# Moving the Winograd operand sums of an attention-plus-MLP kernel from VectorE to GpSimd

## The chip, the cores and the metric

The kernel runs on one core of one Trainium2 chip. The metric is the device time of one execution in microseconds (us); lower is better. The kernel before took 890.3 us in the median of three runs (887.12, 890.3 and 890.57 us). One further execution was recorded with a profile; all rows below are from that one. The engines are called by the profile's short names: PE (TensorE matmul), PEld (its weight loads), DVE (VectorE), ACT (ScalarE), POOL (GpSimd), SP (the queue that issues DMAs here).

## The reference

Attention with softmaxes on q and k apart, then an MLP whose activation is `h * erf(softplus(h))`. Shapes: 8 batches, 8 heads, 576 positions, head size 64; so 4608 tokens of 512 features, and weights of 512x2048 and 2048x512, all float32.

```python
q_s = softmax(q, over d);  k_s = softmax(k, over the sequence)
kv  = einsum('bhsd,bhse->bhde', k_s, v)
x   = einsum('bhsd,bhde->bhse', q_s, kv) as (4608, 512)
h   = x @ w_in
g   = h * erf(max(h, 0) + log1p(exp(-|h|)))
out = g @ w_out
```

## The kernel before, in words

**Tiling.** Tokens are worked in 12 blocks of 384 (three blocks for each pair of batches; `NBK` is 3), and the 2048 hidden features in 4 groups of 512. One item n is a block with a group, so there are 48 items: items 0 to 3 are block 0, items 4 to 7 block 1, items 8 to 11 block 2. Per item, `mm1` makes h for 512 features and 384 tokens, ACT does softplus and erf, DVE multiplies and splits g (lines 933, 946, 950), and `mm2` (line 978) adds to the output tiles.

**Precision.** Block 0 runs in float32 (`mm1_32`, and line 969) while the weights still arrive and are decoded. From block 1 on, each operand is split into a float16 high part and a float16 low part by `split2`: ACT writes the high part (line 268), DVE the low part, from the float32 source and the high part (line 269). Each product then takes three float16 matmuls.

**Seven products in place of eight.** From block 1 on, `mm1` multiplies a 2x2 grid of weight blocks with a 2x2 grid of x blocks in Winograd's form, with seven products (names `pX`, `pY`, `pZ` for the PSUM banks, line 854). For this, sums of the blocks are needed on both sides. On the weights' side `wsplit(jn)` splits the plain blocks A00, A01 and A11, and then line 294 forms four sums in place, each of 128x512 float32, in a chain: A11 = A10 + A11, A10 = A00 - A10, A00 = A11 - A00, A01 = A01 - A00. `wsplit_sums(jn)` splits the four results. This happens once for each of the four groups of `w_in` (jobs 0, 1, 3 and 5 of `JOBS`): 16 sums. On the side of x, `finish(0)` splits the plain blocks of an x block, and `finish(1)` forms four sums in place at line 360, each of 128x384 float32, and splits them: 4 sums for each of blocks 1 to 11, 44 in all. An in-place sum has to come after every split that reads the old value, and the splits of the sums after it.

**Where they stand in the order.** The list `ORDER` gives the sequence in which the program emits its parts, and a planner in the framework lays out each engine's queue from it, so neighbours in a queue can belong to different parts. Each queue is worked in order. After `Z` (the weights' scales) come `S0` (wsplit of job 0), `R0` (wsplit_sums of job 0), `f0 f1` (finish of block 1), `S1 R1`, and later, from `SPLITS`, S3 R3 and S5 R5; S2, S4, S6 and S7 are the splits of `w_out`, which have no sums. Block 2's finish is emitted in item 6. Between them stand the steps of attention for the next batches (`A`), on the same engines.

**Products and what they read.** In `mm1`, part k = 0 reads plain blocks alone; part k = 1 begins with the product that reads weight operand 6 and x operand 3, both sums. DVE also adds the products up in PSUM and SBUF (lines 866, 868, 876, 879), and ACT copies some (871, 873, 881). POOL does little: it clears tiles (lines 105 and 550) and does one subtraction of the first batch (line 740).

Of the kernel before, what the change touches and what calls it, by code (L numbers as in the profile page):

```python
# [13 lines left out]
ALU = mybir.AluOpType  # L14
# [39 lines left out]
def attn_moe_kernel(  # L54
# [9 lines left out]
    nc = tc.nc  # L64
# [15 lines left out]
    NBK = PT // T  # L80
# [122 lines left out]
    def whalf(jn, h):  # L203

        return WT[jn][:, h * 2048:(h + 1) * 2048]

    def wop(jn, h, i, n):

        o = h * WIN + i * 512
        return WT[jn][:, o:o + n * 512].rearrange("p (n c f) -> p n c f", n=n, c=2)  # L210
# [56 lines left out]
    def split2(src, hi, lo, s):  # L267
        nc.scalar.activation(hi, src, AF.Copy, scale=s)  # L268
        nc.vector.scalar_tensor_tensor(lo, src, s, hi, op0=ALU.mult, op1=ALU.subtract)  # L269
# [3 lines left out]
    def wsplit(jn):  # L273


        which, g = wjobs[jn]
        s = w_s[which][:, g:g + 1]
        assert "all" in wready and not raws and jn == nsplit[0]
        nsplit[0] += 1
        if which == "out":  # L280
            split2(stg.pop(jn), whalf(jn, 0), whalf(jn, 1), s)
            wdone(jn)
            return
        sg = stg[jn].rearrange("p (c f) -> p c f", c=4)
        A = {(i, j): sg[:, 2 * j:2 * j + 2, 256 * i:256 * i + 256]
             for i in range(2) for j in range(2)}
        hi, lo = (wop(jn, h, 0, 2).rearrange("p n c f -> p (n c) f") for h in range(2))
        split2(sg[:, :, :256], hi, lo, s)
        split2(A[1, 1], wop(jn, 0, 2, 1)[:, 0], wop(jn, 1, 2, 1)[:, 0], s)
        for o, x, y, op in (  # L290
            ((1, 1), (1, 0), (1, 1), ALU.add), ((1, 0), (0, 0), (1, 0), ALU.subtract),
            ((0, 0), (1, 1), (0, 0), ALU.subtract), ((0, 1), (0, 1), (0, 0), ALU.subtract),
        ):
            nc.vector.tensor_tensor(A[o], A[x], A[y], op=op)

    def wsplit_sums(jn):
        which, g = wjobs[jn]
# [8 lines left out]
    def wdone(jn):  # L306
        wready.add(wjobs[jn])
# [33 lines left out]
    def finish(k):  # L341


        i = x_next[0]
        x = xbl[i]
        Th = T // 2
        if k == 0:
            assert i < 3 or ("m", mm1_last[i - 2], 3) in emitted
            x7[i] = xp.tile([P, 2, 7, 2, Th], F16, tag="x7", name=f"x7_{i}")
            hi, lo = (x7[i][:, h, 0:2].rearrange("p n c t -> p (n c) t") for h in range(2))  # L350
            split2(x[:, :, :Th], hi, lo, 1.0)
            split2(x[:, 2:, Th:], x7[i][:, 0, 2], x7[i][:, 1, 2], 1.0)
            return
        Bk = {(d, j): x[:, 2 * d:2 * d + 2, Th * j:Th * j + Th]
              for d in range(2) for j in range(2)}
        for o, a, b in (
            ((0, 0), (0, 1), (0, 0)), ((0, 1), (1, 1), (0, 1)),
            ((1, 1), (1, 1), (0, 0)), ((1, 0), (1, 0), (1, 1)),
        ):
            nc.vector.tensor_tensor(Bk[o], Bk[a], Bk[b], op=ALU.subtract)  # L360
        for j in range(2):
            hi, lo = (
                x7[i][:, h, 3 + 2 * j:5 + 2 * j].rearrange("p n c t -> p (n c) t")
                for h in range(2)
            )
            split2(x[:, :, Th * j:Th * j + Th], hi, lo, 1.0)
        x_next[0] += 1
# [637 lines left out]
    def tok(name):  # L1005
# [19 lines left out]
        if c == "w":  # L1025
            warm(*x)
        elif c == "D":
            wdecode(NPC * x[0] + x[1])
        elif c == "Q":
            wsquares(*x)  # L1030
        elif c == "S":
            wsplit(*x)
        elif c == "R":
            wsplit_sums(*x)
        elif c == "f":
            xready(x_next[0])
            finish(x[0] % 2)
        elif c == "Z":
            wscales()
        elif c == "m":  # L1040
            (mm1_32 if x[0] < NG else mm1)(*x)
            emitted.add(("m", *x))
        elif c == "M":
            mm2(*x)
            emitted.add(("M", *x))
        else:
            fn[c](*x)
# [82 lines left out]
```

## Time and profile before

| | |
|---|---|
| median of three runs | 890.3 us (887.12 to 890.57) |
| profiled execution: own time | 886.76 us |
| its span, first to last instruction | 884.9 us |
| mean granted TensorE clock | 0.992 of full |
| PE busy | 832.7 us (94%) |
| DVE busy | 656.9 us (74%) |
| ACT busy | 504.5 us (57%) |
| POOL busy | 6.4 us (1%), 14 instructions |

The busy shares are means over stages: the beginning (loads, decoding, block 0), a stage from about 124 to 185 us in which the weights and blocks 1 and 2 are split, and the long rest. The rows below give the stages apart. A stretch of idle time is named with the instruction that ended it.

### The profile page before, as it was taken

The numbers are of one execution on the slowest core, as the hardware profiler recorded it, in microseconds if no ns is written. First come the engines' busy times: TensorE is split into PE (matmuls) and PEld (weight loads), VectorE is DVE, ScalarE is ACT, GpSimd is POOL, SyncE is SP. The second block draws the span as 40 slices with busy tenths as digits, with TensorE's granted clock in tenths as the row PEclk, the third lists the DMA queues.
The fourth block names the chain that finished last, engine by engine and source line by source line (L and its number), as shares of the span: only waits on it lengthen the run. The fifth ranks groups of instructions, "written<-read, shape, count | busy, mean of one in ns | idle before, by whom it ended". The sixth has DMA issues, their size and how long they took to land.

```text
span 884.9 us, 15492 instructions
## 1 busy us (share of the span) xinstructions
PE 832.7 (94%) x6556; PEld 573.0 (65%) x6556; DVE 656.9 (74%) x908; ACT 504.5 (57%) x645; POOL 6.4 (1%) x14
## 2 busy tenths in 40 slices
PE   2899995799989999999999999999999999999997
PEld 1555554566667667767777667667777677676763
DVE  7899589998977796786886596777885575644453
ACT  2468567866475646645745646645745646553632
POOL 2000000000000000000000000000000000000000
PEclk9999998899999999999999999999999999999999
DMA  9983711022104111311033111311010000000100
GB/s 272 361 238 81 224 45 51 2 66 60 49 25 102 48 49 27 89 48 25 13 74 77 37 49 33 76 48 26 13 49 1 13 24 2 24 13 1 36 1 36
DMA packets 117380, 55.52 MB, mean 63 GB/s; under 512 B 106560, under 2 KB 108608, under 8 KB 117312
## 3 DMA queue, kind: packets, MB, share of 16 engines
q1 hardware_dynamic: 117312, 54.54, 22.6%
q8 instruction: 51, 0.84, 0.4%
q14 instruction: 17, 0.14, 0.0%
HBM read 45.09 MB, written 9.44 MB: 62 GB/s over the span
## 4 chain that ended last, share of the span: by engine, by line
PE 65%; DVE 20%; ACT 10%; issue 3%; DMA 1%; SPq 1%; ACTq 0%; DVEq 0%
PE o L978 26%; PE pX L854 14%; PE pZ L854 7%; ACT G L316 5%; ACT L316 4%; PE o L969 3%; PE pY L854 3%; DVE G L933 3%; PE kv L502 3%; PE pX L893 2%; DVE H L950 2%; DVE kmax L458 2%; DVE wt L269 2%; PE qT L577 1%; PE pY L893 1%
## 5 line engine op out<-in xcount | busy, mean ns | idle before, releaser
L978 PE MATMUL o<-wt,H 128*128 128x512 f16 x1584 | 366.1, 379 | 1.9 <-DVE H L946 1.3
L854 PEld LDWEIGHTS <-wt 128*128 128x128 f16 x3696 | 311.5, 98 | 49.1 <-issue 26.3
L978 PEld LDWEIGHTS <-H 128*128 128x128 f16 x1584 | 152.5, 98 | 156.4 <-DVE H L946 1.8
L854 PE MATMUL pX<-x,wt 128*128 128x192 f16 x2112 | 205.9, 247 | 12.6 <-DVE H L876 7.2
L316 ACT ACT_TABLE_LOAD x104 | 133.4, 1283 | 7.0 <-DVE H L879 5.3
L933 DVE SCALAR_TENSOR_TENSOR G<-G,small,H 128x1536 f32<-128x1536 f32 x44 | 80.0, 1818 | 69.3 <-ACT G L316 69.0
L854 PE MATMUL pZ<-x,wt 128*128 128x192 f16 x1056 | 105.5, 249 | 9.3 <-ACT x L268 5.8
L881 ACT COPY H<-pX 128x384 f32<-128x384 f32 x44 | 21.0, 477 | 148.0 <-PE pX L854 143.1
L316 ACT ACTIVATE G<-H,U 128x768 f32<-128x768 f32 (+1 forms) x60 | 73.0, 1232 | 22.7 <-DVE H L879 22.1
L950 DVE TENSOR_TENSOR H<-G,H 128x1536 f16<-128x1536 f32 x44 | 77.3, 1756 | 1.1
L316 ACT ACTIVATE G<-G 128x1536 f32<-128x1536 f32 x48 | 71.2, 1484 | 0.5
L854 PE MATMUL pY<-x,wt 128*128 128x192 f16 x528 | 51.1, 246 | 0.0
L404 ACT ACTIVATE x<-x 128x384 f32<-128x384 f32 (+1 forms) x52 | 17.7, 386 | 55.0 <-PE x L589 52.8
L866 DVE COPY H<-pY 128x384 f32<-128x384 f32 x44 | 24.4, 554 | 30.5 <-PE pY L854 30.5
L946 DVE CAST H<-G 128x1536 f16<-128x1536 f32 x44 | 42.1, 956 | 0.8
L268 ACT ACTIVATE x<-x 128x768 f16<-128x768 f32 (+1 forms) x44 | 33.0, 763 | 15.3 <-DVE x L360 15.3
L269 DVE SCALAR_TENSOR_TENSOR x<-x,x 128x768 f16<-128x768 f32 (+1 forms) x44 | 37.3, 850 | 5.3 <-ACT x L268 5.1
L994 DVE TENSOR_SCALAR ob<-o,V 128x512 f32<-128x512 f32 x29 | 21.7, 748 | 23.8 <-PE o L978 23.8
L879 DVE TENSOR_TENSOR H<-pZ,H 128x384 f32<-128x384 f32 x44 | 24.2, 551 | 18.0 <-PE pZ L854 18.0
L868 DVE TENSOR_TENSOR H<-pX,H 128x384 f32<-128x384 f32 x44 | 24.4, 555 | 14.4 <-PE pX L854 14.2
L360 DVE TENSOR_TENSOR x<-x 128x384 f32<-128x384 f32 x44 | 24.3, 552 | 4.9 <-ACT x L404 4.5
L458 DVE TENSOR_REDUCE kmax<-k 128x256 f32<-128x1024 f32 x14 | 27.6, 1980 | 0.0
(158 smaller groups left out, 814.6 us busy)
## 6 DMA issues: line engine op xcount, KB each, us to landing
out_dram<-ob SPq DMA_DIRECT2D x32, 256.0 KB, 2.2
vbuf<-in_v_dram SPq DMA_DIRECT2D x60, 128.0 KB, 3.0
wt<-in_moe_w_out_dram SPq DMA_DIRECT2D x7, 1024.0 KB, 9.4
q<-in_q_dram SPq DMA_DIRECT2D x56, 128.0 KB, 2.9
k<-in_k_dram SPq DMA_DIRECT2D x56, 128.0 KB, 3.1
wt<-in_moe_w_in_dram SPq DMA_DIRECT2D x5, 1024.0 KB, 8.7
raw<-in_moe_w_in_dram SPq DMA_DIRECT2D x3, 1024.0 KB, 8.6
H_raw<-in_k_dram SPq DMA_DIRECT2D x2, 512.0 KB, 6.5
```

The costliest lines, as they stand in the source:

```text
L268: nc.scalar.activation(hi, src, AF.Copy, scale=s)
L269: nc.vector.scalar_tensor_tensor(lo, src, s, hi, op0=ALU.mult, op1=ALU.subtract)
L316: i = nc.scalar.activation(out_, in_, func, **kw)
L458: nc.vector.tensor_reduce(kmax[:, hf * 4:hf * 4 + 4, :], ks[hf], axis=AX.X, op=ALU.max)
L502: nc.tensor.matmul(bk[a * D:(a + 1) * D, c * W:(c + 1) * W], kk, vv, start=(t == 0), stop=(t == TM),)
L854: nc.tensor.matmul(o, w[wl][:, c, a * P:(a + 1) * P], x[:, xl, xi, c, :], start=(new and a == 0 and c == 0 and i == 0), stop=(c == 1 and i ...
L893: nc.tensor.matmul(ph[:, :T], w[:, c, a * P:(a + 1) * P], x[:, c, :], start=(c == 0), stop=(c == NC4 - 1),)
L933: nc.vector.scalar_tensor_tensor(flat(s["G"]), flat(s["G"]), GA[:, g:g + 1], flat(s["H"]), op0=ALU.mult, op1=ALU.mult,)
L946: nc.vector.tensor_copy(flat(s["gh"]), flat(s["G"]))
L950: nc.vector.tensor_tensor(flat(s["gl"]), flat(s["G"]), flat(s["gh"]), op=ALU.subtract)
L969: nc.tensor.matmul(o, s["G"][:, a, ts_], w[:, a, :], start=(first_ and a == 0), stop=(last_ and a == FG - 1),)
L978: nc.tensor.matmul(o, s[gt][:, a, ts_], w[wl][:, a, :], start=(first_ and a == 0 and i == 0), stop=(last_ and a == FG - 1 and i == 2),)
```

## The change

The four sums on the weights' blocks are done on GpSimd in place of VectorE, in all four groups. The four sums on an x block are done on GpSimd for blocks 1 and 2, and stay on VectorE for blocks 3 to 11. The operands, the order of emission and everything else stay as they are. So 16 instructions of 128x512 and 8 of 128x384 change their engine.

```diff
@@ wsplit
-            nc.vector.tensor_tensor(A[o], A[x], A[y], op=op)
+            nc.gpsimd.tensor_tensor(A[o], A[x], A[y], op=op)
@@ finish
-            nc.vector.tensor_tensor(Bk[o], Bk[a], Bk[b], op=ALU.subtract)
+            (nc.gpsimd if i < NBK else nc.vector).tensor_tensor(
+                Bk[o], Bk[a], Bk[b], op=ALU.subtract
+            )
```

## Rows read from the trace of the kernel before

**Rows 1.** The stretches of the span (us from its start): length, then busy time and instructions of PE, PEld, DVE, ACT and POOL, then the granted clock of PE (1.00 is 2.4 GHz), the share of the DMA engines and GB/s.

```profile
124.00:134.00 10.00, 10.00 (x49) 5.98 (x48) 9.55 (x18) 9.14 (x17) 0.95 (x1) 1.00 0.49 132
134.00:140.00 6.00, 5.09 (x38) 3.38 (x36) 5.95 (x7) 5.27 (x11) 0.95 (x1) 1.00 0.44 117
140.00:148.00 8.00, 1.04 (x6) 0.78 (x6) 8.00 (x12) 5.41 (x7) 0.00 (x0) 0.76 0.06 13
148.00:172.00 24.00, 16.62 (x150) 14.28 (x149) 24.00 (x25) 17.38 (x20) 0.00 (x0) 0.86 0.00 1
...
300.00:500.00 200.00, 196.84 (x1700) 140.24 (x1699) 151.27 (x211) 115.20 (x142) 0.00 (x0) 1.00 0.21 50
```

**Rows 2.** Who waited for whom from 124 to 172 us: engine, line and what it works on, the one waited for, us in total, times, the longest.

```profile
PE pZ L854 <- ACT x L268: 5.8, 1, 5.8
PE pX L854 <- DVE H L876: 3.2, 2, 2.5
...
PE pZ L854 <- DVE x L269: 1.7, 1, 1.7
PE pZ L854 <- ACT H L871: 1.7, 2, 1.1
...
PE pX L854 <- ACT H L873: 1.5, 2, 1.3
```

**Rows 3.** Instructions around block 1's sums in order of time: start, us, engine, line and operation, and in brackets the idle time before it and what ended it.

```profile
138.84 0.85 ACT L404 ACTIVATE x<-x,x_s 128x128 f32<-128x128 f32 x2
...
141.01 0.55 DVE L269 SCALAR_TENSOR_TENSOR x<-x,x 128x384 f16<-128x384 f32 x1
141.48 0.69 DVE L294 TENSOR_TENSOR wt<-wt 128x512 f32<-128x512 f32 x1
...
144.33 0.84 ACT L268 ACTIVATE x<-x 128x768 f16<-128x768 f32 x1 [0.25 <-DVE x L360]
...
146.28 0.95 DVE L269 SCALAR_TENSOR_TENSOR x<-x,x 128x768 f16<-128x768 f32 x1
...
147.28 1.92 PE L854 MATMUL pZ<-x,wt 128*128 128x192 f16 x11 [1.74 <-DVE x L269]
```

**Rows 4.** The chain of work that ended last, the pieces from 110 to 200 us in order of time: start, us, what. Nine pieces of it are line 294 (the first and the last stand here) and three are line 360 (the first and the last).

```profile
130.70 3.33 DMA q<-in_q_dram
...
136.46 0.60 DVE wt L294
...
140.62 0.47 DVE x L360
...
143.83 0.47 DVE x L360
...
169.48 2.09 PE pX L854 x12
...
179.80 0.60 DVE wt L294
```

**Rows 5.** Line 294 and line 360 over the whole span: number, shortest, median and longest duration in ns, first and last start, shape.

```profile
L294 DVE TENSOR_TENSOR wt<-wt x16: 683/685/693, 126.5 to 179.7; 128x512 f32<-128x512 f32 x16
...
L360 DVE TENSOR_TENSOR x<-x x44: 535/552/560, 132.6 to 750.9; 128x384 f32<-128x384 f32 x44
```

**Rows 6.** Instructions at the beginning of the span in order of time, around the one subtraction on POOL.

```profile
8.41 3.81 DVE L458 TENSOR_REDUCE kmax<-H_raw 128x256 f32<-128x1024 f32 x2
8.58 1.90 POOL L740 TENSOR_TENSOR q<-G_raw,q_m 128x1024 f32<-128x1024 f32 x1 [5.38 <-DVE q_m L739]
10.52 1.06 ACT L735 ACTIVATE q<-q 128x1024 f32<-128x1024 f32 x1 [2.19 <-POOL q L740]
```

**Rows 7.** DVE from 124 to 172 us by line and shape: what it writes and reads, number, busy us, mean ns of one, idle time before. Four lines read PSUM and write `H` (866, 868, 876 and 879), with two instructions each; the first and the last of them stand here.

```profile
L269 DVE SCALAR_TENSOR_TENSOR wt<-wt,small,wt 128x1024 f16<-128x1024 f32 x9 | 11.4, 1278 | 0.0
...
L458 DVE TENSOR_REDUCE kmax<-k 128x256 f32<-128x1024 f32 x2 | 4.0, 1990 | 0.0
...
L415 DVE TENSOR_REDUCE q_m<-q 128x16 f32<-128x1024 f32 x1 | 1.2, 1220 | 0.2 <-DMA q<-in_q_dram 0.2
...
L868 DVE TENSOR_TENSOR H<-pX,H 128x384 f32<-128x384 f32 x2 | 1.1, 556 | 0.0
...
L879 DVE TENSOR_TENSOR H<-pZ,H 128x384 f32<-128x384 f32 x2 | 1.1, 552 | 0.0
L946 DVE CAST H<-G 128x1536 f16<-128x1536 f32 x1 | 1.0, 952 | 0.0
...
L472 DVE TENSOR_REDUCE km<-kT 128x4 f32<-128x512 f32 x1 | 0.7, 684 | 0.0
```

**Rows 8.** A later clearing on POOL and the splits that DVE did at that time, in order of time.

```profile
124.39 1.93 DVE L269 SCALAR_TENSOR_TENSOR wt<-wt,small,wt 128x1024 f16<-128x1024 f32 x2
124.46 0.95 POOL L550 MEMSET kvbd<- 128x1024 f16 x1 [113.98 <-DVE Vt L827]
```

**Rows 9.** POOL's first clearing of tiles, when DVE had not begun, by line: number, busy us, mean ns of one.

```profile
L105 POOL MEMSET kvbd<- 128x1024 f16 x2 | 1.9, 952 | 0.0
```

**Rows 10.** PE in order of time in the same stage: two of its groups of twelve matmuls of line 854.

```profile
151.00 1.16 PE L854 MATMUL pX<-x,wt 128*128 128x192 f16 x12
...
172.53 2.13 PE L854 MATMUL pX<-x,wt 128*128 128x192 f16 x12
```

**Rows 11.** The last split that reads the plain blocks of job 1's weights, in the order of time on DVE.

```profile
133.05 0.75 DVE L269 SCALAR_TENSOR_TENSOR wt<-wt,small,wt 128x512 f16<-128x512 f32 x1
```

## The prediction

> **What bounds the kernel now.** I read the time by stretches first [rows 1]. From 300 to 500 us PE is busy 196.84 of 200 us: the rest of the kernel is PE's own work, and whatever is lost before it is added to the end. From 124 to 172 us it is otherwise. From 140 to 148 us PE works 1.04 of 8 us, from 148 to 172 us 16.62 of 24, while DVE is busy 8.00 of 8 and 24.00 of 24. ACT has room there (17.38 of 24). So in this stage one engine, DVE, is full, and it is the stage that holds the changed instructions. The reader should see that DVE's mean over the span (74%) hides this.
>
> The waits say the same from PE's side [rows 2]: 5.8 us for ACT's split of x, 1.7 us for DVE's split of x, 3.2 us for DVE's additions into H, and 1.7 and 1.5 us for ACT's copies of H. The first two are one place: block 1's first product on sums. x of block 1 is complete at 138.84 + 0.85 = 139.69, DVE has still to read it at 141.01, ACT splits the last sums at 144.33, DVE's low part runs from 146.28 to 147.23, and PE goes on at 147.28 [rows 3]. Here DVE works through other things between the steps of one chain.
>
> The chain of work goes almost wholly through DVE from 134 to 169 us; up to 180 us nine pieces of it are line 294 and three are line 360 [rows 4]. Ahead of 134 us it goes through a load of q that ended at 130.70 + 3.33 = 134.03, so DVE's work before that is not what sets the end. Four of the 16 sums on weights, and the first of the four on block 1, lie there [rows 4, 5].
>
> **The change part by part.** Removed from DVE: 16 instructions of 685 ns and 8 of 552 ns [rows 5]. DVE starts the next instruction before the last has ended, so on the chain one counts 0.60 and 0.47 us [rows 4]: 16 x 0.60 + 8 x 0.47 = 13.4 us in all. On the path are 9 x 0.60 + 3 x 0.47 = 6.8 us. The first job's four sums and block 1's first one are hidden behind the load of q, three sums of the last job stand beside softplus and erf on ACT, and block 2's four lie from about 190 us on, where PE has its own work. These twelve give nothing, and cost nothing as long as that cover is there. If PE runs out of work at block 2, its four sums at POOL's price (below) cost at most 4 x (0.71 - 0.47) = 1.0 us.
>
> Added on POOL: the one subtraction of the trace took 1.90 us for 128x1024, with ACT going on 0.04 us after it [rows 6]. By that, 128x512 is 0.95 us and 128x384 is 0.71 us. One takes longer there than on DVE. But POOL does little else in this stage, so the four sums of a job follow one another with nothing between them: 4 x (0.95 + 0.04) = 4.0 us, where job 1's took DVE from 136.46 [rows 4] to 141.48 + 0.69 = 142.17 us [rows 3]. So the splits behind the sums are not late.
>
> No DMA moves. The new waits are at POOL's sums (for the splits that read the old values) and at ACT's splits (for POOL in place of DVE). Behind ACT's split stand its copies of H and softplus; a late sum would hold these up, and then PE.
>
> What the trace doesn't show is a sum on POOL beside an instruction of DVE that reads two SBUF tiles, as the splits do. Its price is bounded thus. Below: nothing. The subtraction on POOL ran beside DVE's reductions, which read one tile, and two of these took 3.81 us [rows 6], against 2 x 1.99 us elsewhere [rows 7]; clearing a tile took 0.95 us beside a split with two inputs [rows 8], as much as when DVE had not begun [rows 9]. Above: while POOL sums, DVE stands still. On the path that would be 9 x 0.95 + 3 x 0.71 = 10.7 us. But part of DVE's work reads one tile or PSUM: 4.0 + 1.2 + 4 x 1.1 + 0.7 + 1.0 = 11.3 us [rows 7] of 9.55 + 5.95 + 8.00 + 24.00 = 47.5 us [rows 1], so 24%; of 10.7 us some 76%, 8.1 us, meet a two-input instruction. I take half of that, 4.1 us, since neither row is the disputed case: one has the operation on POOL without the neighbour on DVE, the other the neighbour without an operation that reads.
>
> Sum: -6.8 + 4.1 = -2.7 us. Ends: -6.8 with nothing paid, +3.9 with all 10.7 us paid.
>
> The profiled execution took 886.76 us, 1.9 us more than its span. The runs shown lie at 887.12, 890.3 and 890.57 us, so the profiled one is 3.5 us under their median. I count from the mean of these four, 888.7 us: 888.7 - 2.7 = 886.0 us. (From the profiled execution alone it is 884.1 us, from the median 887.6 us.)
>
> **The rivals.**
>
> *Nothing is paid, and PE's clock gains too.* DVE gives up 6.8 us and POOL costs it nothing. For this speaks that POOL is idle in the stage and that neither row with POOL at work shows a neighbour stretched [rows 6, 8]. There is a second part: the granted clock fell to 0.76 and 0.86 of full after PE's idle time [rows 1], and twelve matmuls took 2.13 us in place of 1.16 [rows 10], so they ran at the lower of its two levels, 1.2 GHz. Some four such groups stand behind the idle stretches, so up to 4 x 0.97 = 3.9 us could follow. From -6.8 to -10.7 us; I take -8: 880.7 us. Against it speaks that ACT's waits of 1.7 and 1.5 us stay [rows 2].
>
> *DVE and POOL take turns.* Each sum on POOL stops DVE's next two-input instruction, or is stopped by the running one. Then 8.1 us come back for 6.8 us: +1.3 us, 890.0 us, and +3.9 us, 892.6 us, at the upper end. For it speaks only that the stage is full of such instructions (the nine longest splits alone take 11.4 us [rows 7]); no row shows it. The Trainium skill, page "SBUF — State Buffer", section "SBUF: two separate sides", states it as a rule: a VectorE instruction with two SBUF inputs and a GpSimd instruction that reads SBUF contend for a shared pair of ports, which is locked for a whole instruction. No row here tests that; the clearing beside a split [rows 8] reads nothing, and its unchanged 0.95 us agrees with the rule's exception. By the rule the sum would be this rival's.
>
> *POOL's queue makes x late.* This is the case on the other side. POOL works in order. Job 1's sums can begin when their last split has been read, at 133.05 + 0.75 = 133.80 [rows 11]; if they and block 1's three remaining sums stand one behind the other in POOL's queue, seven sums have to be through by 144.3 us, when x's last sum ended before [rows 3]. That decides at (144.3 - 133.8) / 7 = 1.5 us for each. If each waits out a split of DVE (1.28 us [rows 7]) besides its own 0.95 or 0.71, the seven take 4 x 2.23 + 3 x 1.99 = 14.9 us and end at 148.7, 4.4 us late; with another 1 to 2 us for matmuls at the lower clock it is +6: 894.7 us. Against it: between 134 and 140 us DVE has reductions of 1.2 and 2.0 us that read one tile.
>
> *The change doesn't do what it says.* DVE gives up the sums, but the end is then set by the chain through ACT, softplus, erf and the attention of the next batch, and the freed time becomes idle time on DVE. Then 888.7 us.
>
> **How the numbers follow.** Forecast (half paid) 0.36, with its own range 883.5 to 888.5; nothing paid 0.27; turns 0.22; late x 0.10; no effect 0.05. The range reaches from most of the second case to the late x: 880 to 894 us. A measurement of this kernel tells about 0.5%, 4.4 us, from no change. Faster by more: the second case, and a third of the forecast's own case that falls beyond: 0.27 + 0.10 = 0.37. Slower by more: late x and a fifth of the turns: 0.15. The rest, 0.48, is within.
>
> **What would show it.** Right: PE's wait ahead of block 1's pZ falls from 5.8 + 1.7 us by 2 to 3 us, DVE's idle time between 134 and 172 us is no longer nothing, sums on POOL of about 0.95 and 0.71 us, and at most some splits of line 269 stretched. Nothing paid: splits and sums both at their lengths of the rows. Turns: sums on POOL well above 0.95 us, or splits above 1.28 us for 128x1024, with DVE still full. Late x: ACT's split of x waits for POOL beyond 144.3 us. Wrong altogether would be a difference that arises after 200 us, from another order of the queues, which no row can tell beforehand.

## The result, and the profile after

The changed kernel took 897.65 us in the median of six runs (895.81 to 898.47), the kernel before 888.87 us beside it: a ratio of 1.0094 with a 95% interval from 1.0079 to 1.0109, so 8.4 us slower. (Here and below a loss in us is the ratio's, times the median of the kernel before.) The forecast was 886.0 us with a range to 894; the time lies above it. The profiled execution of after took 897.2 us, with a span of 895.0 us. Its lines from 360 on stand two higher than before (404 is now 406, 567 is 569, 854 is 856, 881 is 883).

I read after in the order of the prediction. First the stretches, which answer to [rows 1]: length, busy time and instructions of PE, PEld, DVE, ACT and POOL, granted clock, DMA share, GB/s.

```profile
124.00:134.00 10.00, 7.77 (x30) 4.03 (x29) 7.09 (x9) 5.19 (x9) 7.80 (x5) 1.00 0.40 100
134.00:140.00 6.00, 4.14 (x19) 2.90 (x20) 4.27 (x4) 5.42 (x10) 1.66 (x2) 0.72 0.25 90
140.00:148.00 8.00, 4.28 (x34) 3.03 (x32) 4.97 (x3) 2.91 (x5) 7.76 (x5) 1.00 0.29 66
148.00:172.00 24.00, 9.88 (x88) 8.88 (x88) 17.91 (x16) 14.37 (x18) 12.47 (x8) 0.75 0.00 1
172.00:200.00 28.00, 22.44 (x168) 16.20 (x167) 26.82 (x25) 21.31 (x24) 13.74 (x8) 0.87 0.00 1
300.00:500.00 200.00, 196.37 (x1717) 140.43 (x1716) 151.60 (x214) 114.63 (x140) 0.00 (x0) 1.00 0.20 48
```

The stage from 300 to 500 us is as before: the loss lies ahead of 200 us. In the first four stretches DVE, which was full, is busy only 34.24 of 48 us; PE has gone from 32.75 to 26.08 us and ACT from 37.20 to 27.89. POOL rose from 1.90 to 29.70. DVE, ACT and PE all work less in the same 48 us, so they wait for something. Between 172 and 200 us PE works 22.44 us, where it had 27.27 in the trace of before. Between 148 and 172 us the granted clock is 0.75, where it was 0.86.

The waits from 124 to 180 us, as in [rows 2] (who waited for whom: total us, times, longest):

```profile
ACT wt L268 <- POOL wt L294: 15.4, 4, 5.1
...
PE pZ L856 <- ACT x L268: 11.4, 1, 11.4
DVE wt L269 <- ACT wt L268: 10.9, 5, 3.7
...
PE pX L856 <- ACT H L883: 6.0, 1, 6.0
```

PE's wait of 5.8 us ahead of pZ has become 11.4 us, and a wait for an ACT copy of H has risen to 6.0. Behind both stands ACT, which itself waited 15.4 us for POOL, always with the splits of the weights' sums. How a sum on the weights can make x late is seen in the chain of work, the answer to [rows 4] (start, us, what):

```profile
126.03 1.28 POOL wt L294
127.38 1.88 POOL wt L294
129.33 2.13 POOL wt L294
131.53 1.60 POOL wt L294
133.15 2.19 ACT wt L268 x2
135.34 0.48 ACT qTs L569
135.86 2.01 PE x L588 x2
137.90 0.38 ACT x L406
138.34 1.00 POOL x L360
```

Job 0's four sums take 7.09 us. ACT splits them, and only then copies `qTs`, a tile of attention that has nothing to do with the sums; PE waits for this tile, and x of block 1 comes from PE's product. The reader should see that from the fifth to the sixth piece the link is not data: it is the order of ACT's queue. ACT's own rows show it once more for job 1:

```profile
133.15 2.19 ACT L268 ACTIVATE wt<-wt,small 128x1024 f16<-128x1024 f32 x2 [4.37 <-POOL wt L294]
...
147.59 2.19 ACT L268 ACTIVATE wt<-wt,small 128x1024 f16<-128x1024 f32 x2 [5.09 <-POOL wt L294]
149.68 0.82 ACT L406 ACTIVATE x<-x,x_s 128x128 f32<-128x128 f32 x2
```

The last piece of block 1's x is there at 149.68 + 0.82 = 150.50 us, 10.8 us after the 139.69 of [rows 3]. PE's pZ, at 147.28 in [rows 3] with its eleven matmuls, came at 156.65. In the trace of before one of the two splits of job 0's sums ran ahead of `qTs` (129.03, `qTs` at 130.07) and the other at 132.90, behind it; after, both stand ahead of it. So the queues themselves differ, though the order of emission is the same.

POOL's sums by line and shape from 124 to 200 us, the price that [rows 6] was to give:

```profile
L294 POOL TENSOR_TENSOR wt<-wt 128x512 f32<-128x512 f32 x16 | 28.8, 1799 | 24.8 <-DVE wt L269 23.9
L360 POOL TENSOR_TENSOR x<-x 128x384 f32<-128x384 f32 x8 | 13.0, 1629 | 7.7 <-ACT x L406 6.9 <-DVE x L269 0.6
```

They take 1.80 and 1.63 us, against 0.95 and 0.71 priced. In the chain above the first one of each kind took 1.28 and 1.00 us; others are stretched, and DVE has its own stretched instructions beside them, as in these two rows (an instruction on two tiles that took 0.68 us beside e5's clears, and the split of 128x384 that took 0.55 us in [rows 3]):

```profile
130.25 1.75 DVE L418 TENSOR_TENSOR qt<-qt,qt_m 128x512 f32<-128x512 f32 x1
...
151.17 1.35 DVE L269 SCALAR_TENSOR_TENSOR x<-x,x 128x384 f16<-128x384 f32 x1
```

Against these first lengths the 24 sums took POOL 28.8 - 16 x 1.28 + 13.0 - 8 x 1.00 = 13.3 us longer. DVE lost less: from 124 to 172 us five of its instructions were stretched, by 3.4 us together, and its nine splits of 128x1024 took 1326 ns in the mean, against 1278 in [rows 7]:

```profile
L269 DVE SCALAR_TENSOR_TENSOR wt<-wt,small,wt 128x1024 f16<-128x1024 f32 x9 | 11.8, 1326 | 10.6 <-ACT wt L268 10.6
```

So in the changed kernel it is mostly POOL's results that are late; DVE stands idle for 10.6 us ahead of these splits until ACT has done its part of them.

Three theories follow. **Q**: ACT's queue, through the place of the late sums' splits. **C** (in the last runs **T**): DVE and POOL take turns, and that time is the loss. **U**: POOL is merely slow.

### The profile page after: what moved, and what is told of

Its sections match the earlier page's. It is cut to its first block, busy times and chain, and to the rows that moved or that the text cites. A ratio compares the mean times of both kernels' runs of the same rounds, so it can differ in the third digit from the quotient of the medians.

```text
span 895.0 us, 15502 instructions
## 1 busy us (share of the span) xinstructions
PE 833.4 (93%) x6556; PEld 574.6 (64%) x6556; DVE 652.2 (73%) x884; ACT 504.0 (56%) x645; POOL 48.0 (5%) x38
## 4 chain that ended last, share of the span: by engine, by line
PE 72%; DVE 15%; ACT 6%; POOL 4%; issue 2%; DMA 1%; SPq 0%; ACTq 0%; DVEq 0%; POOLq 0%
PE o L980 30%; PE pX L856 16%; PE pZ L856 8%; PE pY L856 3%; POOL wt L294 3%; PE kv L504 3%; PE o L971 3%; PE pX L895 2%; ACT L316 2%; ACT G L316 2%; DVE kmax L460 2%; DVE H L952 1%; DVE G L935 1%; PE x L591 1%; PE qT L579 1%
## 5 line engine op out<-in xcount | busy, mean ns | idle before, releaser
L856 PE MATMUL pZ<-x,wt 128*128 128x192 f16 x1056 | 105.5, 249 | 11.4 <-ACT x L268 11.4
L269 DVE SCALAR_TENSOR_TENSOR x<-x,x 128x768 f16<-128x768 f32 (+1 forms) x44 | 39.8, 913 | 4.3 <-ACT x L268 4.2
L269 DVE SCALAR_TENSOR_TENSOR wt<-wt,small,wt 128x1024 f16<-128x1024 f32 (+2 forms) x18 | 24.7, 1399 | 10.9 <-ACT wt L268 10.9
L268 ACT ACTIVATE wt<-wt,small 128x1024 f16<-128x1024 f32 (+2 forms) x18 | 20.2, 1144 | 18.5 <-POOL wt L294 18.5
```

The lines of the kernel that those rows point to most:

```text
L856: nc.tensor.matmul(o, w[wl][:, c, a * P:(a + 1) * P], x[:, xl, xi, c, :], start=(new and a == 0 and c == 0 and i == 0), stop=(c == 1 and i ...
```

## The experiments

The kernel before ran beside each group of runs; its median was 888.34 us for the first four, 888.97 for the next four, 889.51 for the last four.

**One part alone.** The weights' sums on POOL and x's on DVE; then the other way round.

```diff
-            (nc.gpsimd if i < NBK else nc.vector).tensor_tensor(
+            nc.vector.tensor_tensor(
                 Bk[o], Bk[a], Bk[b], op=ALU.subtract
```

> Line 294's 16 sums on GpSimd, line 360 all on VectorE. Theory Q (ACT's queue: the splits of the weights' sums wait for POOL, and the attention copies queued behind them, and so block 1's x, are late): nearly the whole loss, +6 to +9 us against before, and PE's wait ahead of block 1's first pZ of 9 to 12 us as in the changed kernel. Theory C (shared access to SBUF: sums on POOL and two-input instructions of DVE stop each other, and DVE's lost time is the loss): two thirds of the loss, 16 of 24 sums, +5 to +6 us. Theory U (POOL is merely slow: 1.27 us for a sum in place of 0.95): +3 us.

898.42 us, ratio 1.0108 (1.0094 to 1.0122). The weights' sums alone lose 9.6 us, the whole loss and more, and more than any of the theories gave. x was complete at 147.67 us, so it was late, but PE's longest wait for ACT's split of it was 6.3 us, and not the 9 to 12 of Q.

```diff
-            nc.gpsimd.tensor_tensor(A[o], A[x], A[y], op=op)
+            nc.vector.tensor_tensor(A[o], A[x], A[y], op=op)
```

> Line 360's 8 sums of blocks 1 and 2 on GpSimd, line 294 on VectorE. Q: no copy of attention stands behind a wait for these sums, so -1 to +1.5 us, and x of block 1 complete at about 140 us as before. C: a third of the loss, +2.5 to +3.5 us. That x's sums were late in POOL's queue behind the weights' (the rival of the prediction): no loss here, since the queue holds nothing else.

894.95 us, 1.0069 (1.0055 to 1.0083): 6.1 us slower, above what either theory gave. The two parts' losses don't add up to the whole. Here x was nearly in time (complete at 140.56 us, against 139.69 in [rows 3]), and still pZ waited 11.2 us. DVE, POOL and ACT show why:

```profile
139.74 4.29 DVE L269 SCALAR_TENSOR_TENSOR wt<-wt,small,wt 128x1024 f16<-128x1024 f32 x2
143.94 0.54 DVE L269 SCALAR_TENSOR_TENSOR x<-x,x 128x384 f16<-128x384 f32 x1
```

```profile
L269 DVE SCALAR_TENSOR_TENSOR wt<-wt,small,wt 128x2048 f16<-128x2048 f32 x1 | 3.1, 3090 | 0.0
```

```profile
140.23 1.64 POOL L360 TENSOR_TENSOR x<-x 128x384 f32<-128x384 f32 x1 [1.08 <-ACT x L406]
144.63 4.91 POOL L360 TENSOR_TENSOR x<-x 128x384 f32<-128x384 f32 x2 [2.76 <-DVE x L269]
```

```profile
149.57 1.58 ACT L268 ACTIVATE x<-x 128x768 f16<-128x768 f32 x2 [3.52 <-POOL x L360]
```

The first row merges two splits: one of 128x1024, which kept its 1.28 us, and one of 128x2048 (the third row, by shape), which took 3.09 us, against 2.35 in the trace of before. Only 0.74 us of the 4.29 are turns. The rest is order: the planner put both ahead of the small split of x, which in the trace of before ran at 141.01 [rows 3], with the split of 128x2048 behind it, from 147.14 us. The small split reads what POOL's next sum overwrites, so this sum was late, and two sums took 4.91 us where they take 2.0 alone. ACT's split came at 149.57, where it was 144.33 [rows 3].

**ACT's queue put right.** The splits of the sums of jobs 0 and 1 are held on ACT behind the last copy of block 1's x, with `R0` emitted after `f1`; `issue_after` fixes this place in the queue.

```diff
-    A A f0 f1 U3 S1 R1 M3.0 M3.1 M3.2 S2
+    A A f0 f1 U3 S1 R0 R1 M3.0 M3.1 M3.2 S2
...
+                if jn < 2:
+                    es.enter_context(tc.issue_after(lastx[0]))
```

> The changed kernel, but the splits of jobs 0 and 1's sums are issued on ACT behind the last copy of block 1's x (emitted later, and tied to that copy in ACT's queue). All 24 sums stay on GpSimd. Q: x of block 1 is complete near 140 us again, ACT waits for POOL with nothing of attention behind it, and the loss falls from 8.8 to between 0 and +4 us. C: the same sums beside the same splits, so the loss stays at +6 to +9 us.

895.9 us, 1.0082 (1.0068 to 1.0096). The edit did what it should: x was complete at 138.6 us. The loss is still 7.3 us, because the next queue took over. On POOL, x's sums stand behind job 1's, and ACT waits for them (two views, POOL and ACT):

```profile
137.23 4.96 POOL L295 TENSOR_TENSOR wt<-wt 128x512 f32<-128x512 f32 x3
...
143.04 5.43 POOL L364 TENSOR_TENSOR x<-x 128x384 f32<-128x384 f32 x3
```

```profile
147.43 0.84 ACT L268 ACTIVATE x<-x 128x768 f16<-128x768 f32 x1 [6.35 <-POOL x L364]
```

Q alone falls. Its control is the same hold with all sums on DVE:

```diff
-    A A f0 f1 U3 S1 R1 M3.0 M3.1 M3.2 S2
+    A A f0 f1 U3 S1 R0 R1 M3.0 M3.1 M3.2 S2
...
-            nc.gpsimd.tensor_tensor(A[o], A[x], A[y], op=op)
+            nc.vector.tensor_tensor(A[o], A[x], A[y], op=op)
```

> The kernel before, all sums on VectorE, with the splits of jobs 0 and 1's sums issued on ACT behind the last copy of block 1's x, as in e3. What the held splits do by themselves: both theories -1.5 to +2 us; the loss of e3 is to be read against this one.

888.63 us, 0.9995 (0.998 to 1.0011). The hold itself costs and brings nothing.

**The contention by itself.** The kernel before, with 16 more additions on POOL that nobody waits for, from 124 us on. All else is as before.

```diff
+        dm = cp.tile([P, 512], F16, name="dm")
+        for _ in range(16):
+            nc.gpsimd.tensor_tensor(dm, sg[:, :512], sg[:, 512:1024], op=ALU.add)
```

> The kernel before with all sums on VectorE, and besides 16 additions on GpSimd from about 124 us on, of 128x512 float32 from two SBUF tiles into a scratch tile that nobody reads. The queues of the other engines are as before, instruction for instruction. Q and U: no one waits for them, so 0 +- 1.5 us, and splits of 128x1024 at 1.28 us. C: splits and additions beside each other are stretched by up to the other's length; about 15 us of additions meet two-input instructions, +4 to +10 us.

901.91 us, 1.0140 (1.0122 to 1.0157): 12.4 us slower (10.8 to 13.9, above the 4 to 10 of C) by additions on which nothing depends. POOL in order of time, and then DVE from 126.64 to 152.9 us by line and shape (busy us, mean ns), where lines are five higher:

```profile
124.50 1.28 POOL L270 TENSOR_TENSOR dm<-sg 128x512 f16<-128x512 f32 x1
...
126.64 26.33 POOL L270 TENSOR_TENSOR dm<-sg 128x512 f16<-128x512 f32 x15
```

```profile
L299 DVE TENSOR_TENSOR wt<-wt 128x512 f32<-128x512 f32 x7 | 11.0, 1567 | 0.0
L274 DVE SCALAR_TENSOR_TENSOR wt<-wt,small,wt 128x1024 f16<-128x1024 f32 x4 | 7.8, 1960 | 0.0
L274 DVE SCALAR_TENSOR_TENSOR wt<-wt,small,wt 128x512 f16<-128x512 f32 x2 | 3.5, 1755 | 0.0
L274 DVE SCALAR_TENSOR_TENSOR x<-x,x 128x768 f16<-128x768 f32 x1 | 2.0, 2016 | 0.0
L463 DVE TENSOR_REDUCE kmax<-k 128x256 f32<-128x1024 f32 x1 | 2.0, 1957 | 0.0
L365 DVE TENSOR_TENSOR x<-x 128x384 f32<-128x384 f32 x1 | 1.6, 1615 | 0.0
L420 DVE TENSOR_REDUCE q_m<-q 128x16 f32<-128x1024 f32 x1 | 1.2, 1206 | 0.0
```

By shape, DVE's instructions that read two tiles lost 0.7 to 1.07 us in the mean; the two reductions, which read one tile, lost nothing (1990 and 1220 ns in [rows 7]). Single ones differ. A split of 128x1024 lost up to 1.01 us (DVE in order of time):

```profile
137.65 2.29 DVE L274 SCALAR_TENSOR_TENSOR wt<-wt,small,wt 128x1024 f16<-128x1024 f32 x1
```

The one that began at 145.88 us, as an addition had just ended, kept its 1.27 us, and the next addition took 2.23: either side can be the one that waits. Against the lengths of [rows 3, 5, 7, 11] DVE lost 7 x 0.88 + 4 x 0.68 + 2 x 1.0 + 1.07 + 1.06 = 13.0 us. The time rose by 12.4: in this stage DVE's loss is the end's loss, about one for one. U can't explain this run, since nobody uses these additions. The Trainium skill (page "SBUF — State Buffer", section "SBUF: two separate sides") has as a rule that of such a pair the one that starts first holds the shared ports for its whole instruction, and the other waits. The trace agrees that one waits for the other; in length it comes close and no more, since no DVE instruction lost more than 1.07 us to an addition that takes 1.28.

**Which of POOL's accesses does it?** In place of the 16 additions: 40 clears (no reading), and 16 multiplications by 1.0 that read one tile.

```diff
-            nc.gpsimd.tensor_tensor(dm, sg[:, :512], sg[:, 512:1024], op=ALU.add)
+            nc.gpsimd.memset(dm, 0.0)
```

> As e4, with 40 clears of the scratch tile (some 20 us) in place of the 16 additions: POOL writes and doesn't read. T: 0 +- 1.5 us, splits at 1.28 us for 128x1024. If any work on POOL slows DVE (a shared write side, or power and clock): +4 us or more.

890.26 us, 1.0007 (0.9991 to 1.0023). DVE's splits, from 124 to 149 us, are as long as in [rows 7], and its sums (686 ns) as in [rows 5]:

```profile
L274 DVE SCALAR_TENSOR_TENSOR wt<-wt,small,wt 128x1024 f16<-128x1024 f32 x6 | 7.7, 1277 | 0.0
```

```diff
-            nc.gpsimd.tensor_tensor(dm, sg[:, :512], sg[:, 512:1024], op=ALU.add)
+            nc.gpsimd.tensor_scalar(dm, sg[:, :512], 1.0, None, op0=ALU.mult)
```

> As e4, with 16 multiplications by 1.0 that read one SBUF tile of 128x512 float32 and write the scratch tile. If it is reading on POOL that takes turns with DVE's two-input instructions, as the Trainium skill's rule has it: DVE's splits are stretched again, by the length of these shorter instructions, +3 to +12 us. If only a second input on POOL meets DVE's second input: 0 +- 1.5 us.

892.9 us, 1.0037 (1.0023 to 1.0051), 3.3 us slower, in between. DVE's sums from 124 to 156 us:

```profile
L301 DVE TENSOR_TENSOR wt<-wt 128x512 f32<-128x512 f32 x8 | 7.9, 983 | 0.0
```

Reading one tile on POOL costs DVE 0.30 us in the mean for a sum of 0.69. No DVE instruction from 124 to 156 us lost more than 0.44 us, though the multiplication takes 1.50 us alone (it is not the shorter instruction that its expectation takes it for), so DVE waited for a part of it only. Writing alone cost these splits and sums nothing.

**The same additions where PE sets the end.** The 16 additions at 386 us.

```diff
+        if b == 4:
...
+            for _ in range(16):
+                nc.gpsimd.tensor_tensor(dm, sg[:, :512], sg[:, 512:1024], op=ALU.add)
```

> As e4 (16 additions on GpSimd into a tile that nobody reads, all other queues as before), but started when the scales of batch 4 are known, where PE is busy 98% and DVE 75%. T: instructions of DVE with two SBUF inputs are stretched as in e4, by about 1 us each, but PE sets the end there: 0 to +4 us, against +13.6 us in e4.

889.67 us, 1.0007 (0.9992 to 1.0022). The turns are taken there as well (POOL by line, then the stretch from 380 to 420 us):

```profile
L567 POOL TENSOR_TENSOR dm<-wt 128x512 f16<-128x512 f32 x16 | 25.0, 1565 | 1.3
```

```profile
380.00:420.00 40.00, 39.62 (x313) 27.78 (x312) 31.60 (x40) 18.74 (x28) 25.28 (x17) 1.00 0.15 40
```

The additions took 1.57 us each in place of 1.28, but PE is busy 39.62 of 40 us and DVE has room, so nothing is lost.

**The hand-over without the reading.** The changed kernel with each sum replaced by 2.5 clears of its result, which take about as long as a sum alone (0.52 + 0.52 + 0.31 us). The sums are left out.

```diff
-            nc.gpsimd.tensor_tensor(A[o], A[x], A[y], op=op)
+            nc.gpsimd.memset(A[o], 0.0)
+            nc.gpsimd.memset(A[o], 0.0)
+            nc.gpsimd.memset(A[o][:, :, :128], 0.0)
```

> The changed kernel, with each of the 24 sums on GpSimd replaced by clears of the same result (two and a half of it, about as long as a sum): they wait for the same splits and are waited for by the same splits, but read nothing. It leaves out the sums, so the products on them are of zeros. Theory T (turns: a sum on POOL and a two-input instruction of DVE stop each other): no split is stretched, DVE has given up 6.8 us on the path, and the time is 3 to 8 us under before. Theory Q (ACT's splits wait for POOL with attention's copies behind them): the waits of ACT for POOL and the loss stay, +5 to +9 us.

875.98 us, 0.9843 (0.9821 to 0.9865): 14.0 us faster than before, more than the 3 to 8 of T, and so 22.4 us faster than the changed kernel. The stretch from 124 to 172 us, and DVE's splits in it:

```profile
124.00:172.00 48.00, 41.19 (x300) 30.48 (x300) 46.12 (x51) 42.85 (x56) 22.02 (x53) 0.93 0.17 45
```

```profile
L269 DVE SCALAR_TENSOR_TENSOR wt<-wt,small,wt 128x1024 f16<-128x1024 f32 x12 | 15.1, 1276 | 0.2 <-ACT wt L268 0.2
```

PE works 41.19 of 48 us (32.75 before), and DVE and ACT are nearly full. So DVE does set the end in this stage, and giving up the sums pays where POOL doesn't get in its way. The 22.4 us are not turns alone: the planner laid out other queues here than in the changed kernel, a clear waits for fewer instructions than a sum, which also reads the result of the one before it, and what the zeros do to PE's time was not tried.

**What is left with ACT's queue right and x's sums on DVE.** e1 with the hold of e3.

```diff
-            (nc.gpsimd if i < NBK else nc.vector).tensor_tensor(
+            nc.vector.tensor_tensor(
...
+                if jn < 2:
+                    es.enter_context(tc.issue_after(lastx[0]))
```

> Line 294's 16 sums on GpSimd, block 1's and 2's sums back on VectorE, and the splits of jobs 0 and 1's sums held behind the last copy of block 1's x. So neither attention's copies on ACT nor x's sums on POOL stand behind a sum on weights. Theory T (turns, by the length of a sum): the splits and x's sums on DVE beside POOL's sums are still stretched, by some 1 us each, and the loss is +3 to +9 us. Theory Q (queues only): the loss is gone, -3 to +1.5 us.

893.9 us, 1.0054 (1.0039 to 1.0068). Half of e1's loss is gone, so ACT's queue has a share. The rest lies in T's range and not in Q's, but it is not turns alone either: the splits of job 3 were not held, and there the next wait came up (ACT in order of time):

```profile
160.47 1.15 ACT L268 ACTIVATE wt<-wt,small 128x1024 f16<-128x1024 f32 x1 [3.17 <-POOL wt L295]
164.09 1.15 ACT L268 ACTIVATE wt<-wt,small 128x1024 f16<-128x1024 f32 x1 [2.47 <-POOL wt L295]
...
165.97 0.46 ACT L877 COPY H<-pZ 128x384 f32<-128x384 f32 x1
```

PE waited 6.85 us for this copy, to 166.48.

**The sums that were to cost nothing.** Only job 5's sums and block 2's are on POOL: eight of the twelve that the prediction put off the path.

```diff
-            nc.vector.tensor_tensor(A[o], A[x], A[y], op=op)
+            (nc.gpsimd if jn == 5 else nc.vector).tensor_tensor(A[o], A[x], A[y], op=op)
...
-            (nc.gpsimd if i < NBK else nc.vector).tensor_tensor(
+            (nc.gpsimd if i == 2 else nc.vector).tensor_tensor(
```

> Only job 5's four sums and block 2's four on GpSimd, those that run after about 170 us, all others on VectorE. T: turns are taken, but where PE has its own work; -1 to +3 us. If a sum on GpSimd costs the same wherever it runs (8.8 us for 24 sums, 8 of them here): +3 us.

894.69 us, 1.0068 (1.0050 to 1.0085): 6 us slower, more than expected. POOL, ACT and PE in order of time:

```profile
175.04 6.78 POOL L294 TENSOR_TENSOR wt<-wt 128x512 f32<-128x512 f32 x3 [35.60 <-DVE wt L269]
```

```profile
184.03 2.19 ACT L268 ACTIVATE wt<-wt,small 128x1024 f16<-128x1024 f32 x2 [5.42 <-POOL wt L294]
...
187.53 1.06 ACT L316 ACTIVATE k<-k 128x1024 f32<-128x1024 f32 x1
```

```profile
188.64 0.97 PE L504 MATMUL kv<-vbuf,k 128*64 128x65 f32 x16 [4.37 <-ACT k L316]
```

Three sums took 6.78 us, ACT stood behind them for 5.42, and the exponentials of k behind it held up PE for 4.37 us. From 172 to 200 us PE worked 23.63 us where it had 27.27.

**Is it only DVE's order?** No POOL at all: DVE's first reductions of batch 2 are held behind block 1's last low split, so that x's chain goes first.

```diff
+            if b == 2:
+                es.enter_context(tc.issue_after(lastlo[0]))
```

> No sum on GpSimd. The kernel before, with the first maxima of batch 2's k and q on DVE issued behind the last low split of block 1. It asks what a microsecond of DVE's queue ahead of block 1's x is worth: 3.2 us of reductions leave the place between 134 and 146 us. If DVE's queue there sets PE's wait: -1.5 to -4 us. If DVE's whole work up to 171 us sets the end, in whatever order: -1 to +1 us.

891.01 us, 1.0017 (1.0007 to 1.0027). That is 1.5 us slower (0.6 to 2.4), just above the second range. Nothing is gained; PE then waits 6.4 us at another product for ACT's split of x. So this change of DVE's order moved the wait and didn't remove it.

No version that computes the reference's result was faster than before beyond its interval.

## Why the prediction was wrong, step by step

**DVE sets the end of this stage** [rows 1 to 4]: right. e4 shows 13.0 us lost on DVE and 12.4 lost at the end; e5 shows 14 us gained. That a loss before 200 us goes whole to the end was right too (300 to 500 us is unchanged).

**"On the path are 9 x 0.60 + 3 x 0.47 = 6.8 us"**: undersized, by what e5 shows. Its 14.0 us (12.0 to 15.9) are close to the 13.4 us of all 24 sums, as the prediction worked them out. That the twelve others count in full is not shown by itself, since e5 has other queues and a higher clock (0.996 over its span) as well.

**"By that, 128x512 is 0.95 us and 128x384 is 0.71 us"**: too low; the measured ones are more than a third longer. Alone they take 1.28 us (e4's first) and 1.00 us (the chain above). [rows 6] was a poor measure: line 740 subtracts `q_m`, a tile of maxima (128x16 in [rows 7]), so its second input is a small tile read again and again. Whether that alone makes it cheaper was not tried.

**"I take half of that, 4.1 us"**: mis-sized for a full DVE. e4's DVE lost 13.0 us beside 16 additions that take 16 x 1.28 = 20.5 us alone, of which 3.2 us ran beside the two reductions: 13.0 of 17.3, three quarters and not half. By the prediction's own sum with the measured prices: 9 x 1.28 + 3 x 1.00 = 14.5 us, times 0.76 times 0.75 is 8.3, less 6.8: +1.5 us. That is an estimate, and it has the sign right, but not the size. In the changed kernel DVE lost only 3.4 us in this way, since it was no longer full. What the sum left out is the other side: the 13.3 us by which POOL's sums were stretched stand in it at nothing.

**"So the splits behind the sums are not late"**: the step that failed. It set 4.0 us for a job's four sums; they took 7.09, 8.26 and 8.28 us (e1: 7.09, 6.38 and 8.28). At 1.28 us each, with the 0.08 between two of them, four would take 5.4; the rest is stretching. The text then named what stands behind ACT's split (copies of H, softplus), but gave it no price, and it left out attention's copies `qTs` and x, which were the first to be hit. After shows ACT 15.4 us idle there; e3 and e9 show that this is one wait in a row of several: with ACT's queue mended, POOL's queue (e3) or the next job's copy of H (e9) is late.

**"These twelve give nothing, and cost nothing"**, with at most 1.0 us for block 2: wrong. Eight of them alone cost 6 us (e10), through the same queue. Job 0's sums were to be hidden behind a load of q; after, they start the chain above.

**The rivals.** The turns exist, as that rival had them, but it priced them at +1.3 to +3.9 us, as if no one waited for the sums. The late x came true in the changed kernel, 10.8 us and not 4.4 late. Its decision point, 1.5 us for a sum, was passed (1.80), but the place was first ACT's queue and only then POOL's. "Nothing is paid" would be right for an instruction on POOL that doesn't read (e7, e5). Of what was to show right or wrong, the prediction had "sums on POOL well above 0.95 us" for turns, which came, "with DVE still full", which did not: DVE was idle for 13.8 of 48 us, 10.6 of them waiting for ACT's splits of the weights' sums. Two slips there changed little: a third of 0.36 is 0.12 and not 0.10, and the nine splits called the longest are of 128x1024, where one of 128x2048 takes 2.35 us.

**Together**: taking turns makes both engines slow, which is shown without any hand-over (e4). The hand-over then puts the stretched sums into the chain, where in-order queues on ACT and POOL hold up work that doesn't need them (after, e3, e9, e10). The granted clock from 148 to 172 us is lower besides (0.75 against 0.86); its share was not measured by itself. What share of the 8.4 us each has stays open: the parts don't add (e1 and e2 alone lost 9.6 and 6.1 us), and every edit to the queues uncovers another wait.

## What to carry to other kernels

Before an operation that reads two tiles is moved from a full VectorE to an idle GpSimd, read what VectorE does at that time: if it, too, reads two tiles, the two took turns in these runs, and the move gave back what it saved and more. Then list what stands in the in-order queue behind the first instruction that waits for the moved result, needed or not, and price that at the stretched length. The contention can be measured without the change: run the operation idle on GpSimd beside the unchanged kernel, once where VectorE is full and once where it isn't.

## What the runs showed of the hardware

- A POOL addition of two float32 tiles of 128x512 took 1.28 us alone and 1.68 us in the mean beside a full DVE (e4); DVE's own sum of that size went from 0.69 to 1.75 us at most, and a split of 128x1024 from 1.28 to 2.29 at most.
- Clears on POOL cost DVE's splits and sums nothing (40 of 0.525 us, e7). A POOL multiplication that reads one tile took 1.50 us alone, more than the addition of two, yet cost the kernel only 3.3 us, where the additions cost 12.4.
- DVE's reductions from one tile, and its copies from PSUM, kept their lengths beside POOL's additions (1957, 1206 and 545 ns in e4).
- A conversion on DVE of 128x1536 from float32 to float16, which reads one tile, did not: in e3 one took 1.76 us beside POOL's sums, against 0.95 in [rows 7]. Beside it even a clear had to wait: in e5 the clear of 128x512 that began during a conversion, at 163.83 us, took 1.27 us and not 0.52.
